# Raw score products of the second batch moved ahead of the first FFN tile, with fixed engine and load orders there

## The chip, the cores and the metric

The kernel runs on one core of a Trainium2 chip, in one launch. The metric is the device time of that launch in microseconds (us). The engines are PE (TensorE), DVE (VectorE), ACT (ScalarE), POOL (GpSimd) and SP (SyncE, which here only issues transfers).

## The reference

A channel attention is followed by a two-layer network. For each of 4 batches, q, k and v are 6080 x 256:

```python
qn = q / (np.linalg.norm(q, axis=1, keepdims=True) + 1e-06)
kn = k / (np.linalg.norm(k, axis=1, keepdims=True) + 1e-06)
s = kn.transpose(0, 2, 1) @ qn / tau          # 256 x 256 per batch
a = np.exp(s - s.max(-1, keepdims=True))
a /= a.sum(-1, keepdims=True) + 1e-09
x = (v @ a).reshape(24320, 256)
h = x @ w_in                                   # 256 -> 2048
return np.maximum(0.01 * h, h) @ w_out         # 2048 -> 256
```

The two weights arrive as 64-bit floats, which the kernel takes apart as pairs of 32-bit integers.

## The kernel before

**Stages.** The attention matrix of a batch is folded into the first weight: for each batch the kernel makes W = a w_in (256 x 2048), and then computes v W, the leaky step and the product with w_out. In the text, "batch 1" is the first one and "batch 2" the second (`scores[0]` and `scores[1]` in the code, b = 0 and b = 1).

**Scores.** q and k of a batch are read in 48 chunks of 128 rows, two to a group (`G = 2`, 24 groups; `Scores.load`, L124). A chunk's product k^T q adds into one PSUM bank (`product`, L168). It has two forms. Raw: the float32 chunk goes into the matmul as it is, two matmuls, each of which the trace shows as two records. Split: ScalarE rounds the chunk to a shorter format (`cast`, L157), VectorE takes what is left (`low`, L162), and six matmuls multiply high and low halves. Beside it each chunk is squared on ScalarE (`square`, L151) and added up on VectorE (`add_square`, L154), for the norms. When all chunks are in, a chain follows: sums, norms, rows, scaling, exponentials, transposes (`norms_mm` to `turned_low`).

**Weights.** A block of 128 x 512 64-bit numbers is converted (`f64_split`, L320) by six VectorE and three ScalarE instructions, with the loads in `Conversions.load`. There are 8 blocks of w_in and 8 of w_out. Converted w_in blocks are also stored to memory for later batches (L371). `w_product` (L395) multiplies a column block j of w_in by the attention matrix (two times six matmuls), `w_taken` copies it to SBUF, and `w_parts` (L417) forms the sums and the high and low halves of the stationary blocks for pairs 2j and 2j+1.

**FFN tiles.** The 6080 columns of a batch's v are cut into 6 tiles (five of 1024 columns, as two halves of 512, and one of 960), 24 tiles in all; tile 0 is the first tile of batch 1. A tile runs over 8 pairs p of the hidden blocks. A pair is a Strassen-Winograd step of seven block products of three matmuls (`block_product`, L546), with copies of PSUM to SBUF on ScalarE (`taken`, L574), additions on VectorE (`add`, L569) and the leaky step with its split into halves (`leaky`, L557). The 24 matmuls with w_out for a pair (`ffn_out`, L583) are spread through the next pair by `out(n)`. v is split by `v_parts` (L520) one tile ahead.

**Order.** A tile framework orders the instructions of each engine; `in_order` (L99) adds an edge from the last instruction that was noted for an engine. In the tile loop (L854) the main sequence is written out; side work is put in queues by engine (`put`, L630) and taken out by `slot(queue, room)` (L621): as many entries as their given lengths fit into the room. `at(w, fn)` attaches work to pair number w of the whole run. A batch's score chunks (`chunk_work`, L652) are attached while the batch before is in its tiles.

**The start before.** All 24 groups of batch 1 are multiplied raw, with four weight conversions in between (L787 to L796). Then the first 5 groups of batch 2 (`FILL = 5`, 10 chunks) are multiplied raw and squared while the chain of batch 1's softmax runs (L797 to L842), with no order between most of these steps beyond the ones that `issue_after` states; v of tile 0 is split; W's first column block is made. The other 12 conversions are attached to pairs 0 to 5, two to each, as whole runs (`convert`, L741), and column blocks 1 to 3 of W to pairs 0 to 5 (`w_early`, L698). The remaining 38 chunks of batch 2 take the split form, spread over 25 pairs from pair 8 on (L752 to L758).

**Buffers.** `v_split` (10 buffers) holds the raw groups of batch 1, early w_in blocks and v's halves; `g_split` (5) squares and later the leaky halves; `qk_split` (3) two square sums and later chunk halves; `w_split` (4) W's blocks for one pair each; `raw` (4) 64-bit blocks, raw groups and w_in blocks.

Of the kernel before, what the change touches and what calls it, by code (L numbers as in the profile page):

```python
# [19 lines left out]
G = 2  # L20
# [3 lines left out]
FILL = 5  # L24
# [7 lines left out]
def channel_attention_ffn(  # L32
# [77 lines left out]
    class Scores:  # L110
# [78 lines left out]
        def sums(self):  # L189

            acc, other = self.acc
            nc.vector.tensor_tensor(out=acc, in0=acc, in1=other, op=ALU.add)
            nc.vector.tensor_tensor(out=acc[:, :, 0, :], in0=acc[:, :, 0, :], in1=acc[:, :, 1, :], op=ALU.add)
            self.acc = [acc[:, :, 0, :]]

# [118 lines left out]
    def f64_load(bits):  # L314

        raw = ld.tile([P, TW, 2], I32, name="f64_raw", tag="raw", bufs=RBUFS)
        nc.sync.dma_start(out=raw.rearrange("p n w -> p (n w)"), in_=bits.bitcast(I32))
        return raw

    def f64_split(raw, hi, lo):  # L320
        low, high = raw[:, :, 0], raw[:, :, 1]
        scale, x = temp(I32, "f64_scale"), temp(I32, "f64_x")
        nc.vector.tensor_scalar(
            out=scale, in0=high, scalar1=20, scalar2=0x7FF, op0=ALU.logical_shift_right, op1=ALU.bitwise_and
        )
        nc.vector.tensor_scalar(out=x, in0=high, scalar1=0xFFFFF, scalar2=None, op0=ALU.bitwise_and)
        nc.scalar.activation(out=scale, in_=scale, func=AF.Relu, bias=exp_bias[:, 0:1], scale=2.0**23)
        tail = low.bitcast(F32)
        nc.scalar.activation(out=tail, in_=low.bitcast(U32), func=AF.Copy, scale=2.0**-52)
        nc.vector.scalar_tensor_tensor(  # L330
            out=scale, in0=high, scalar=-(2**31), in1=scale, op0=ALU.bitwise_and, op1=ALU.bitwise_or
        )
        x32 = x.bitcast(F32)
        nc.vector.scalar_tensor_tensor(out=x32, in0=x, scalar=2.0**-20, in1=tail, op0=ALU.mult, op1=ALU.add)
        nc.vector.scalar_tensor_tensor(
            out=x32, in0=x32, scalar=1.0, in1=scale.bitcast(F32), op0=ALU.add, op1=ALU.mult
        )
        nc.scalar.copy(out=hi, in_=x32)
        nc.vector.tensor_tensor(out=lo, in0=x32, in1=f32(hi), op=ALU.subtract)

    class Conversions:
# [5 lines left out]
        def load(self):  # L347
            bits, split = self.blocks.pop(0)
            self.loaded.append((f64_load(bits), split))

        def split(self):
            raw, split = self.loaded.pop(0)
            split(raw)
# [3 lines left out]
    win = {}  # L357
# [9 lines left out]
    def win_block(j, h, early):  # L367
        def split(raw):
            w = win[j, h] = win_tile(early)
            f64_split(raw, w[:, 0, :], w[:, 1, :])  # L370
            nc.sync.dma_start(out=win_dram[j][h], in_=flat(w))  # L371

        return w_in[h * P:(h + 1) * P, j * TW:(j + 1) * TW], split
# [41 lines left out]
    w_sums = {}  # L415

    def w_parts(b, j):  # L417
# [25 lines left out]
        for k in range(2):  # L443
# [24 lines left out]
            def rest(k=k, p=p, blocks=blocks, store=store):  # L468
                last = split(k, blocks(S1, 4, "w_rest"), S1, (s12, S1, 2), (s34, S3, 2))
                store(S1, 4)  # L470
                if b == 0:
# [18 lines left out]

    def wo_block(i):
        fs = slice(i * FPB, (i + 1) * FPB)

        def split(raw):
            f64_split(raw, *(wo[x][:, fs, :].rearrange("p f d -> p (f d)") for x in range(2)))

        return w_out.rearrange("(f p) d -> p f d", p=P)[:, fs, :], split
# [5 lines left out]
    def v_load(i):  # L503
# [3 lines left out]
        src = vT[b].rearrange("(h p) n -> p h n", p=P)[:, :, t * TILE:t * TILE + 2 * w]  # L507
        for h in range(CH):
            nc.sync.dma_start(out=raw[:, h, :, 0:w], in_=src[:, h, :].rearrange("p (j n) -> p j n", j=2))
        v_raw[i] = raw  # L510
# [72 lines left out]
    def ffn_out(i, p):  # L583
# [4 lines left out]
        f1 = f2 + 2  # L588
        if p == 0:
# [62 lines left out]
    def chunk_work(sc, j):  # L652
# [4 lines left out]
        if j == 0:  # L657
            sc.begin([acc_tile()], bank("s"))
            put("act", 0.6, lambda: sc.square(0, sc.acc[0]))
# [37 lines left out]

    def w_early(j, h):  # L698


        def taken():
            ins = w_taken(0, j, h)
            if h == CH - 1:
                for _, fn in w_parts(0, j):
                    with in_order("dve"):
                        issued["dve"] = fn()
            return ins

        put("pe_late", 1, lambda: w_product(0, j, h, "y"), [("act", 0.6, taken, (), True)])

# [11 lines left out]
    for i in range(NTILES):  # L722
        w = i * NPAIR
        if i + 1 < NTILES:
            at(w, v_load, i + 1)
            at(w + 2, v_begin, i + 1)
            at(w + 4, v_work, i + 1, 2, 7)
            at(w + 7, v_work, i + 1, 7, 11, True)
# [7 lines left out]
    win_blocks = [[win_block(j, h, j < 2) for h in range(CH)] for j in range(NWC)]  # L736
    conv = Conversions(win_blocks[0] + win_blocks[1] + [
        x for j in range(NWC) for x in wo_blocks[2 * j:2 * j + 2] + (win_blocks[j + 2] if j + 2 < NWC else [])
    ])

    def convert(n):  # L741
        for _ in range(n):
            conv.load()
        for _ in range(n):
            conv.split()

    for w in range(6):
        at(w, convert, 2)
    for b in range(1, B):
        w0 = (b - 1) * WPB  # L750
        sc = scores[b]
        done = FILL * G if b == 1 else 0  # L752
        begin_at, span = (NPAIR, 25) if b == 1 else (2, 31)
        when = {j: w0 + begin_at + (j - done) * span // (NCHUNK - done) for j in range(done, NCHUNK)}
        for i in range(done // G, len(sc.groups)):
# [18 lines left out]
    def load_ahead(i):  # L774
        if i < n0:
            after["load"] = sc.load(i, work.tile([P, 2, G, C], F32, name="qk_raw0", tag="v_split", bufs=VBUFS))
            with tc.issue_after(after["load"].ins):
                if i in EARLY_LOAD:
                    conv.load()
                if i == n0 - 1:  # L780
                    v_load(0)
# [5 lines left out]
    for i in range(n0):  # L787
# [5 lines left out]
        for j in sc.groups[i]:  # L793
            sc.product(j)
        if i in EARLY_SPLIT:
            conv.split()  # L796
    sc.sums()  # L797
    sc.norms_mm()
    sc.norms_taken()
    sc.norms_begun()  # L800
    after["dve"] = sc.norms()
    with tc.issue_after(after["load"].ins):
        for i in range(min(2, FILL)):
            nxt.load(i, qk_raw())
    sc.rows_mm()
    sc.rows_taken()
    after["scaled"] = sc.scaled()
    sc.exps()
    after["normed"] = sc.normed()
    nxt.begin([acc_tile()], bank("s"))  # L810
    filled = []

    def fill(n):
        for i in range(len(filled), min(len(filled) + n, FILL)):
            for j in nxt.groups[i]:
                nxt.product(j)
                if j == 0:
                    nxt.square(j, nxt.acc[0])
                else:
                    sq = temp(name="sq").rearrange("p (x c) -> p x c", x=2)  # L820
                    nxt.square(j, sq)
                    nxt.add_square(sq)
            if i + 2 < FILL:
                nxt.load(i + 2, qk_raw())
            filled.append(i)

    with tc.issue_after(after["dve"].ins):
        fill(2)
    sc.turn("x")
# [96 lines left out]
```

## Time and profile before

| what | value |
|---|---|
| median of 3 runs | 2223.62 us (2222.81 to 2224.13) |
| the profiled execution, first to last instruction | 2225.9 us |
| its mean granted TensorE clock | 0.990 |
| PE busy | 2174.0 us (98%) |
| DVE busy | 1488.5 us (67%) |
| ACT busy | 1483.2 us (67%) |
| first copy of tile 0's outputs (ACT, L609) | 209.4 us after the start |
| mean DMA rate | 146 GB/s |

The page is one execution, seen by the hardware profiler. Busy time is the union of an engine's instructions, and a busy PE need not be at full rate: the granted clock stands in a line of its own. In the page's second part the span is cut in 40 slices, and each digit is a busy share in tenths. A group of instructions has its line, engine, form, count, busy time, mean length in ns, and the idle time of the engine ahead of it with what ended it. A table of stages has for each stretch the length, the busy time of PE, its weight loads (PEld), DVE, ACT and POOL with the count of instructions, the granted clock, the share of the DMA engines and GB/s. In the list of waits stand the total, the count and the longest.

### The profile page before, as it was taken

The numbers are of one execution on the slowest core, as the hardware profiler recorded it, in microseconds if no ns is written. First come the engines' busy times: TensorE is split into PE (matmuls) and PEld (weight loads), VectorE is DVE, ScalarE is ACT, GpSimd is POOL, SyncE is SP. The second block draws the span as 40 slices with busy tenths as digits, with TensorE's granted clock in tenths as the row PEclk, the third lists the DMA queues.
The fourth block names the chain that finished last, engine by engine and source line by source line (L and its number), as shares of the span: only waits on it lengthen the run. The fifth ranks groups of instructions, "written<-read, shape, count | busy, mean of one in ns | idle before, by whom it ended". The sixth has DMA issues, their size and how long they took to land.

```text
span 2225.9 us, 27253 instructions
## 1 busy us (share of the span) xinstructions
PE 2174.0 (98%) x9940; PEld 1814.1 (81%) x9940; DVE 1488.5 (67%) x2651; ACT 1483.2 (67%) x2563; POOL 2.8 (0%) x10
## 2 busy tenths in 40 slices
PE   9679999999999999999999999999999999999999
PEld 7467888888888888888887888888888888888887
DVE  7986667666766776666766667676677655556554
ACT  6556777766657777776656777777665666666665
POOL 0000000000000000000000000000000000000000
PEclk9889999999999999999999999999999999999999
DMA  9435343342753434433464344343354432332331
GB/s 347 145 142 200 121 155 134 130 157 83 241 204 112 156 123 145 154 116 138 147 227 156 119 159 159 115 155 129 121 192 156 146 137 83 138 121 100 119 118 36
DMA packets 98967, 324.74 MB, mean 146 GB/s; under 512 B 10257, under 2 KB 22033, under 8 KB 98833
## 3 DMA queue, kind: packets, MB, share of 16 engines
q1 hardware_dynamic: 98832, 323.00, 42.1%
q8 instruction: 78, 1.28, 0.2%
q14 instruction: 57, 0.46, 0.1%
HBM read 264.50 MB, written 58.46 MB: 145 GB/s over the span
## 4 chain that ended last, share of the span: by engine, by line
PE 89%; DVE 5%; DMA 3%; ACT 2%; issue 0%; SPq 0%; ACTq 0%; DVEq 0%
PE ps_o L597 44%; PE ps_x L551 22%; PE ps_z L551 11%; PE ps_y L551 5%; PE ps_s L182 5%; PE ps_s L401 1%; DMA qk_raw<-in_k_dram 1%; DVE h L572 1%; DVE g_split L565 1%; DMA w_dram<-w_rest 1%; ACT h L562 1%; ACT g_split L563 1%; DMA f_raw<-in_w_out_dram 1%; DMA qk_raw<-in_q_dram 1%; DVE v_split L516 0%
## 5 line engine op out<-in xcount | busy, mean ns | idle before, releaser
L597 PE MATMUL ps_o<-g_split,w_out_split 128*128 128x512 f32 (+1 forms) x4608 | 1165.5, 388 | 0.0
L597 PEld LDWEIGHTS ps_o<-g_split,w_out_split 128*128 128x128 f32 x4608 | 867.7, 188 | 175.5
L565 DVE TENSOR_TENSOR g_split<-h,g_split 128x512 fp32r<-128x512 f32 (+1 forms) x768 | 525.0, 684 | 395.3 <-ACT g_split L563 394.4
L551 PE MATMUL ps_x<-v_split,w_split 128*128 128x512 f32 (+1 forms) x2304 | 653.7, 392 | 29.4 <-DVE w_split L439 16.2
L562 ACT ACTIVATE h<-h 128x512 f32<-128x512 f32 (+1 forms) x576 | 361.8, 628 | 292.3 <-DVE h L572 292.3
L578 ACT COPY h<-ps_x 128x512 f32<-128x512 f32 (+1 forms) x576 | 334.3, 580 | 312.4 <-PE ps_x L551 311.7
L551 PEld LDWEIGHTS ps_x<-v_split,w_split 128*128 128x128 f32 x2304 | 423.7, 189 | 114.0 <-ACT h L578 12.4
L563 ACT CAST g_split<-h 128x512 fp32r<-128x512 f32 (+1 forms) x768 | 473.4, 616 | 23.9
L572 DVE TENSOR_TENSOR h<-ps_z,h 128x512 f32<-128x512 f32 (+1 forms) x384 | 262.0, 682 | 284.7 <-ACT h L578 278.0
L551 PE MATMUL ps_z<-v_split,w_split 128*128 128x512 f32 (+1 forms) x1152 | 324.4, 390 | 6.3 <-DVE h L572 6.3
L551 PEld LDWEIGHTS ps_z<-v_split,w_split 128*128 128x128 f32 x1152 | 216.5, 188 | 52.5 <-DVE h L572 8.1
L551 PE MATMUL ps_y<-v_split,w_split 128*128 128x512 f32 (+1 forms) x576 | 162.9, 391 | 0.6 <-ACT w_a L411 0.6
L572 DVE TENSOR_TENSOR h<-ps_y,h 128x512 f32<-128x512 f32 (+1 forms) x192 | 131.3, 684 | 0.6
L551 PEld LDWEIGHTS ps_y<-v_split,w_split 128*128 128x128 f32 x576 | 109.0, 190 | 23.5 <-ACT w_a L411 1.1
L182 PEld LDWEIGHTS ps_s<-qk_split 128*128 128x128 f32 x804 | 114.1, 190 | 11.3 <-issue 1.0
L562 ACT ACTIVATE h<-ps_x 128x512 f32<-128x512 f32 (+1 forms) x192 | 112.8, 587 | 10.8 <-PE ps_x L551 10.8
L182 PE MATMUL ps_s<-qk_split 128*128 128x256 f32 x804 | 118.1, 283 | 0.0
L160 ACT CAST qk_split<-qk_raw 128x512 fp32r<-128x512 f32 x134 | 82.9, 619 | 31.8 <-PE ps_s L182 24.0
L516 DVE TENSOR_TENSOR v_split<-v_raw,v_split 128x512 fp32r<-128x512 f32 (+1 forms) x144 | 98.7, 686 | 4.7
L155 DVE TENSOR_TENSOR sq_acc<-sq_acc,sq 128x512 f32<-128x512 f32 x141 | 96.2, 683 | 0.0
L164 DVE TENSOR_TENSOR qk_split<-qk_raw,qk_split 128x512 fp32r<-128x512 f32 x134 | 91.6, 684 | 2.3 <-ACT qk_split L160 2.3
L152 ACT ACTIVATE sq<-qk_raw 128x512 f32<-128x512 f32 x141 | 88.8, 633 | 2.0 <-DMA qk_raw<-in_k_dram 2.0
(101 smaller groups left out, 726.7 us busy)
## 6 DMA issues: line engine op xcount, KB each, us to landing
w_split<-w_dram SPq DMA_DIRECT2D x184, 896.0 KB, 4.7
qk_raw<-in_q_dram SPq DMA_DIRECT2D x92, 256.0 KB, 3.6
qk_raw<-in_k_dram SPq DMA_DIRECT2D x92, 256.0 KB, 3.8
v_raw<-in_vT_dram SPq DMA_DIRECT2D x40, 512.0 KB, 4.9
out_dram<-o_sb SPq DMA_DIRECT2D x80, 256.0 KB, 4.2
win<-win_dram SPq DMA_DIRECT2D x24, 512.0 KB, 4.1
w_dram<-w_rest SPq DMA_DIRECT2D x24, 512.0 KB, 3.1
w_dram<-w_first SPq DMA_DIRECT2D x24, 384.0 KB, 3.4
```

The lines of the kernel that those rows point to most:

```text
L152: return nc.scalar.activation(out=out, in_=self.chunk(j), func=AF.Square)
L155: return nc.vector.tensor_tensor(out=self.acc[0], in0=self.acc[0], in1=sq, op=ALU.add)
L164: return nc.vector.tensor_tensor(out=sp[:, :, 1, :], in0=self.chunk(j), in1=f32(sp[:, :, 0, :]), op=ALU.subtract)
L182: mm = nc.tensor.matmul(out=s, lhsT=lhsT, rhs=rhs, start=False, stop=last and n == len(passes) - 1, skip_group_check=True,)
L516: last = nc.vector.tensor_tensor(out=sp[:, 1, 0:w], in0=src, in1=f32(sp[:, 0, 0:w]), op=ALU.subtract)
L551: mm = nc.tensor.matmul(out=ps[:, 0:n], lhsT=w[:, x, a, :], rhs=sp[:, y, 0:n], start=first and k == 0, stop=k == 2, skip_group_check=True,)
L562: nc.scalar.activation(out=out[:, 0:n], in_=h[:, 0:n], func=AF.Prelu, alpha=0.01)
L563: issued["act"] = nc.scalar.copy(out=sp[:, 0, 0:n], in_=out[:, 0:n])
L565: issued["dve"] = nc.vector.tensor_tensor(out=sp[:, 1, 0:n], in0=out[:, 0:n], in1=f32(sp[:, 0, 0:n]), op=ALU.subtract)
L572: issued["dve"] = nc.vector.tensor_tensor(out=h[:, 0:n], in0=ps[:, 0:n], in1=h[:, 0:n], op=ALU.add)
L578: issued["act"] = nc.scalar.copy(out=h[:, 0:n], in_=ps[:, 0:n])
L597: issued["pe"] = nc.tensor.matmul(out=o_ps[i][j][h][:, 0:n], lhsT=wo[x][:, f, h * P:(h + 1) * P], rhs=sp[:, y, 0:n], start=p == 0 and earl ...
```

## The change

- `FILL` goes from 5 to 18: 36 chunks of batch 2 are multiplied raw ahead of tile 0. Their loads go to buffers that are unused at that time (`spare`), in a fixed order on SP with v and the weight blocks.
- The last 12 chunks of batch 2 are multiplied raw too, in tile 0: five in pair 0, one in each later pair.
- No chunk of batch 2 is squared ahead of tile 0. Its 48 squares are taken from a second load of q and k, in 25 pairs from pair 8 on; nothing is cast, subtracted or multiplied there.
- Order of the start: a helper `run` puts each instruction behind the last one on its engine, so that VectorE, ScalarE, PE and SP there have the order that is written.
- A conversion becomes seven steps (`f64_steps`). At the start they are interleaved by hand for six blocks (the first four of w_out and w_in's third column block); in tile 0 the last six are queue entries, each step putting the next.
- W's column block 1 is multiplied ahead of tile 0 and cut in its queue; blocks 2 and 3 are made in pairs 0 and 1 and pairs 3 and 4. Their parts are queued in the order `FIRST`, which puts pair 2j's first half ahead of the sums.
- Stores of the four early w_in blocks wait in a list: one is issued in the middle of the start, three behind the last loads.
- In v's split for tile 0 the cast goes to ScalarE. In tile 0 alone the slots have more room.

The diff, cut to its core (`FIRST` is (2, 0, 1, 3, 4, 5)):

```diff
-FILL = 5
+FILL = 18
...
+    def run(engine, fn, *args):
+        with in_order(engine):
+            issued[engine] = ins = fn(*args)
+        return ins
...
+        return [("dve", 0.85, fields), ("act", 0.72, power), ("act", 0.7, floats), ("dve", 0.7, sign),
+                ("dve", 1.4, value), ("act", 0.65, upper), ("dve", 0.7, lower)]
...
+        def store():
+            w = win[j, h] = win_new[j, h]
+            stores.append(lambda: nc.sync.dma_start(out=win_dram[j][h], in_=flat(w)))
+            if j > 1:
+                stores.pop()()
...
-        nc.vector.tensor_copy(out=sp[:, 0, 0:w], in_=src)
+        if i:
+            nc.vector.tensor_copy(out=sp[:, 0, 0:w], in_=src)
+        else:
+            with in_order("act"):
+                issued["act"] = nc.scalar.copy(out=sp[:, 0, 0:w], in_=src)
...
+                parts = list(w_parts(0, j))
+                if j == 2:
+                    for x in FIRST:
+                        put("dve", *parts[x])
+                else:
+                    run("dve", parts[FIRST[0]][1])
+                    for x in reversed(FIRST[1:]):
+                        put("dve", *parts[x], (), True)
...
-    for j in range(1, NWC):
+    for j in range(2, NWC):
         for h in range(CH):
-            at(2 * j - 2 + h, w_early, j, h)
+            at(3 * j - 6 + h, w_early, j, h)
...
-    for w in range(6):
-        at(w, convert, 2)
+    for w in (0, 0, 2, 3, 4, 5):
+        at(w, convert, w > 0)
...
-        for j in range(done, NCHUNK):
-            at(when[j], chunk_work, sc, j)
+        for j in range(NCHUNK):
+            at(when[j], square_work if b == 1 else chunk_work, sc, j)
...
+    def spare(i):
+
+        if i < 3:
+            t = work.tile([P, 2, NS, P], F32, name="qk_raw1", tag="w_split", bufs=4)
+            return t.rearrange("p x s f -> p (x s f)")[:, 0:2 * G * C].rearrange("p (x g c) -> p x g c", x=2, g=G)
+        if i < 8 or 11 <= i < 16:
+            return work.tile([P, 2, G, C], F32, name="qk_raw1", tag="g_split", bufs=GBUFS)
+        return work.tile([P, 2, G, C], F32, name="qk_raw1", tag="qk_split", bufs=3)
...
+    fill(3)
+    run("dve", sc.sums)
+    run("pe", sc.norms_mm)
+    conv_begin()
+    conv_do(0, 2)
+    run("dve", sc.norms_taken)
...
+    run("pe", sc.turn, "x")
+    conv_do(0)
+    v_do(1)
+    run("sp", stores.pop(0))
+    run("act", sc.turned_high)
...
+    for h in range(CH):
+        run("pe", w_product, 0, 1, h, "yz"[h])
+        run("act", w_taken, 0, 1, h)
+    v_do(3)
+    conv_do(3, 2)
+    conv_begin()
+    conv_do(4, 2)
+    conv_do(3)
+    fill(2)
+    v_do(5)
+    conv_do(4, 2)
+    conv_begin()
+    conv_do(5, 2)
+    conv_do(4)
+    fill_load(1)
+    fill(1)
+    parts = list(w_parts(0, 1))
+    for x in FIRST:
+        put("dve", *parts[x])
+    conv_do(5, 3)
+    fill_load(3)
+    while stores:
+        run("sp", stores.pop(0))
+    for j in range(FILL * G, NCHUNK):
+        w = max(0, j - NCHUNK + NPAIR)
+        if w and j % G == 0:
+            at(w - 1, lambda i=j // G: nxt.load(i, spare(i)))
+        at(w, put, "pe", 1, lambda j=j: nxt.product(j))
...
-            slot("act", 0.65)
+            slot("act", 0.65 if i else 0.75)
...
-            slot("pe", 1)
+            slot("pe", 1 if i or p else 3)
...
-            slot("dve", 2.2)
+            slot("dve", 2.2 if i else 3.6)
...
-            slot("act", 1.8)
+            slot("act", 1.8 if i else 2.2)
...
-            slot("dve", 1.3)
+            slot("dve", 1.3 if i else 2.8)
...
+            if i == 0:
+                slot("dve", 1.5)
```

More of the change, by code (lines that the diff above doesn't have):

```diff
@@ L367, in win_block, with halves @@
     def win_block(j, h, early):
[L368 to L373, printed above, removed]
+        def halves():
+            w = win_new[j, h] = win_tile(early)
+            return w[:, 0, :], w[:, 1, :]
+        def store():
[3 more added lines that the diff above has]
+                stores.pop()()
+        return w_in[h * P:(h + 1) * P, j * TW:(j + 1) * TW], halves, store
     def win_load(j):
@@ L413, in w_taken @@
         return ins
-    w_sums = {}
+    w_done = set()
     def w_parts(b, j):
@@ L470, in rest @@
                 store(S1, 4)
+                w_done.add((b, p))
                 if b == 0:
@@ L775, in load_ahead @@
         if i < n0:
[L776 to L781, printed above, removed]
+            run("sp", sc.load, i, work.tile([P, 2, G, C], F32, name="qk_raw0", tag="v_split", bufs=VBUFS))
+            if i in EARLY_LOAD:
+                run("sp", conv.load)
     for i in range(AHEAD):
@@ L793, in channel_attention_ffn @@
         for j in sc.groups[i]:
-            sc.product(j)
+            issued["pe"] = sc.product(j)
         if i in EARLY_SPLIT:
             conv.split()
[L797 to L809, printed above, removed]
@@ L811, in channel_attention_ffn, with fill_load @@
+    def fill_load(n):
+        for i in range(len(nxt.raw), len(nxt.raw) + n):
+            run("sp", nxt.load, i, spare(i))
     filled = []
     def fill(n):
-        for i in range(len(filled), min(len(filled) + n, FILL)):
+        for i in range(len(filled), len(filled) + n):
             for j in nxt.groups[i]:
[L816 to L824, printed above, removed]
-            filled.append(i)
@@ L827, in channel_attention_ffn @@
[L827 to L842 removed]
+                run("pe", nxt.product, j)
@@ new lines, in fill, with conv_begin, conv_do, v_do @@
+            filled.append(i)
+    running = []
+    def conv_begin():
+        running.append(deque(conv.steps()))
+    def conv_do(n, steps=1):
+        for _ in range(steps):
+            engine, _, fn = running[n].popleft()
+            run(engine, fn)
+            while running[n] and running[n][0][0] == engine:
+                run(engine, running[n].popleft()[2])
+    def v_do(n):
+        for fn in v_tile[:n]:
+            run("dve", fn)
+        del v_tile[:n]
+    fill_load(4)
+    run("sp", v_load, 0)
@@ new lines, in channel_attention_ffn @@
+    v_tile = [fn for _, fn in v_parts(0)]
+    fill_load(1)
+    run("sp", conv.load)
+    fill_load(2)
+    run("sp", conv.load)
+    fill(3)
[4 more added lines that the diff above has]
+    run("dve", sc.norms_taken)
+    run("dve", sc.norms_begun)
+    run("dve", sc.norms)
+    fill(3)
+    fill_load(2)
+    run("sp", conv.load)
+    run("pe", sc.rows_mm)
+    conv_begin()
+    conv_do(1, 2)
+    run("dve", sc.rows_taken)
+    run("dve", sc.scaled)
@@ new lines, in channel_attention_ffn @@
+    conv_do(1)
+    v_do(1)
+    fill(2)
+    fill_load(2)
+    run("sp", conv.load)
+    parts = [list(w_parts(0, j)) for j in (0,)]
+    for x in FIRST:
+        run("dve", parts[0][x][1])
+    conv_do(2, 2)
+    conv_begin()
+    conv_do(3, 2)
+    conv_do(2)
+    fill(2)
+    fill_load(2)
+    for h in range(CH):
+        run("pe", w_product, 0, 1, h, "yz"[h])
+        run("act", w_taken, 0, 1, h)
+    v_do(3)
+    conv_do(3, 2)
+    conv_begin()
+    conv_do(4, 2)
+    conv_do(3)
+    fill(2)
```

155 lines of the change are left out of this document (92 added, 63 removed).

## The prediction

> **What bounds the kernel now.** I read the page first, then a table of stages whose borders I set at three events: the end of batch 1's score products, the first FFN product, and the first product of the second tile. The page gives the span and shows that TensorE idles, and loses its clock, only near the start:
>
> ```profile
> span 2225.9 us, 27253 instructions
> ...
> PE   9679999999999999999999999999999999999999
> ...
> DVE  7986667666766776666766667676677655556554
> ...
> PEclk9889999999999999999999999999999999999999
> ```
>
> A slice is 55.6 us; slices two to four (up to 223 us) are where PE is below 9, and DVE is fullest there. The table of stages (length, then busy time of PE, PEld, DVE, ACT, POOL, the granted clock, DMA share and GB/s):
>
> ```profile
> 0.00:48.70 48.70, 44.61 (x195) 38.01 (x195) 36.72 (x48) 33.47 (x38) 1.75 (x8) 1.00 0.97 346
> 48.70:77.50 28.80, 17.72 (x71) 13.47 (x71) 26.91 (x67) 12.65 (x25) 0.00 (x0) 0.86 0.54 191
> 77.50:202.40 124.90, 98.83 (x373) 74.54 (x374) 100.89 (x218) 70.87 (x122) 0.00 (x0) 0.88 0.44 158
> 202.40:292.90 90.50, 90.50 (x431) 76.09 (x430) 61.84 (x100) 67.44 (x118) 0.00 (x0) 1.00 0.41 138
> 1740.00:1821.60 81.60, 81.60 (x361) 67.35 (x360) 48.32 (x78) 52.91 (x92) 0.00 (x0) 1.00 0.35 119
> ```
>
> I call the five rows A to E. A: batch 1's raw scores; DMA share 0.97, PE nearly full. B: the softmax chain, 28.8 us, in which PE works 17.7 and DVE 26.9: VectorE and the dependency chain set its length. C: tile 0 takes 124.9 us with DVE busy 100.9 (81%) and PE at a clock of 0.88. D: the second tile, 90.5 us, PE without a gap. E: a tile of the last batch, which has no score work beside it, 81.6 us, again without a gap. So from 202.4 us on a microsecond of TensorE work is a microsecond of time; before that it is not.
>
> Who holds PE in C, from the waits there:
>
> ```profile
> PE ps_x L551 <- DVE w_split L439: 16.2, 4, 5.3
> PE ps_x L551 <- ACT h L578: 7.2, 7, 1.9
> PE ps_x L551 <- DVE w_split L440: 5.0, 3, 3.0
> ```
>
> 21 us are waits for VectorE to cut the weights that the next pair needs. VectorE also does most of eleven of the sixteen weight conversions in this tile (the count of L335 below).
>
> **Part 1: products leave tiles 1 to 4.** Before, 38 of batch 2's 48 chunks are cast, subtracted and multiplied as six matmuls in pairs 8 to 32. Now only their squares stay there. Price of one product, from the timeline of TensorE in the second tile (start, length, instruction), and of one three-matmul block:
>
> ```profile
> 226.76 0.88 PE L182 MATMUL ps_s<-qk_split 128*128 128x256 f32 x6
> 227.47 0.86 PE L551 MATMUL ps_x<-v_split,w_split 128*128 128x512 f32 x3
> ...
> 233.23 0.84 PE L551 MATMUL ps_x<-v_split,w_split 128*128 128x512 f32 x3
> 233.91 0.84 PE L551 MATMUL ps_z<-v_split,w_split 128*128 128x512 f32 x3
> ```
>
> From start to start a product is 0.71 us, so 38 are 27.0. The other way: D minus E is 8.9 us for 8 pairs; over the 25 pairs that is 27.8. I take 27.4. All of it lies on PE in stretches where PE has no gap, so it counts in full. What is next late there? In E VectorE is busy 48.3 of 81.6 us; all 48 squares over the same 25 pairs are 15 a tile, one ScalarE and one VectorE instruction each, against 12 chunks with two and two now, so both stay below D's 67.4 and 61.8. The squares' inputs are read a second time: D's DMA share is 0.41, and its score loads grow from 12 to 15 chunks. No cost. Term: -27.4.
>
> **Part 2: the fill before tile 0 grows from 10 chunks to 36.** A raw chunk is four records; from the long run in A, 42.77 us for 48 chunks, a group of two costs 1.78 us:
>
> ```profile
> 5.55 42.77 PE L182 MATMUL ps_o<-qk_raw 128*128 128x256 f32 x192
> 48.70 1.10 PE L173 MATMUL ps_s<-qk_raw,zeros 128*128 128x512 f32 x2 [0.37 <-DMA qk_raw<-in_k_dram]
> ...
> 77.47 0.77 PE L551 MATMUL ps_x<-v_split,w_split 128*128 128x512 f32 x1 [3.93 <-DVE w_split L439]
> ```
>
> 18 groups are 32.1 us. Two column blocks of weights (24 matmuls at 0.227, a third of the 0.68 between the last two rows above) are 5.4; before, only one block was made here. The small products (zeros, norms, rows, transposes) are between 0 and 6.1: B's 17.72 less five groups (8.9) and twelve weight matmuls (2.7), the upper end holding the cold clock; I take 4. Sum 41.5: PE runs 48.7 to 90.2 if fed, so tile 0 starts 12.7 us later than its 77.5.
>
> Is it fed? Loads first, from the SyncE timeline, the issue table and a window of A:
>
> ```profile
> 41.42 0.47 SPq L129 DMA_DIRECT2D qk_raw<-in_q_dram  x1
> ```
> ```profile
> qk_raw<-in_q_dram SPq DMA_DIRECT2D x92, 256.0 KB, 3.6
> ```
> ```profile
> 20.00:40.00 20.00, 20.00 (x95) 17.60 (x94) 19.16 (x27) 15.95 (x20) 0.52 (x1) 1.00 1.04 389
> ```
>
> A group is q and k, 512 KB. 18 groups, six weight blocks, the first tile of v and one store are 14.2 MB, 36.4 us at 389 GB/s: done near 78 when begun at 41.4, while PE wants the last at 88. A group comes every 1.35 us and is eaten every 1.78. The three remaining stores, put last on SP, wait behind the load of group 20, which needs the buffer of group 17 (about 90); one weight tile of the conversions waits for the first of them, to about 95, when VectorE would reach it anyway. So PE is the bound of the fill.
>
> VectorE in this stretch, by lengths of single instructions in C (and, from its timeline, the sums that begin the chain of the norms):
>
> ```profile
> L565 DVE TENSOR_TENSOR g_split<-h,g_split 128x512 fp32r<-128x512 f32 x31 | 21.3, 687 | 10.8 <-ACT g_split L563 10.8
> L335 DVE SCALAR_TENSOR_TENSOR f_x<-f_x,f_scale 128x512 f32<-128x512 f32 x11 | 7.4, 683 | 0.0
> L440 DVE TENSOR_TENSOR w_split<-w_s,w_split 128x256 fp32r<-128x256 f32 x16 | 6.0, 416 | 0.0
> L516 DVE TENSOR_TENSOR v_split<-v_raw,v_split 128x512 fp32r<-128x512 f32 x7 | 4.8, 691 | 0.2
> L323 DVE TENSOR_SCALAR f_scale<-f_raw 128x512 int32<-128x512 int32 x10 | 4.2, 421 | 1.0 <-DMA f_raw<-in_w_out_dram 1.0
> L439 DVE CAST w_split<-w_s 128x256 fp32r<-128x256 f32 x16 | 3.9, 284 | 0.0
> ```
> ```profile
> 50.86 1.22 DVE L192 TENSOR_TENSOR sq_acc<-sq_acc,sq_acc 128x1024 f32<-128x1024 f32 x1
> ```
>
> A conversion is two of 0.42 and four of 0.68: 3.6. Cutting one column block is about 6.9 (four sums at 0.42, then eight casts and eight subtractions between 0.22 and 0.42; mean about 0.33). The v splits of tile 0 without their casts, now on ScalarE, are 11 at 0.69: 7.6. Six conversions 21.4, one block 6.9, v 7.6, and the score chain about 10.5 (estimate: B's 26.9 less the v parts, squares and conversion steps now in it): 46.4 from 50.9, so VectorE is through at about 97.5. That is 7 us after PE has finished the fill. PE has pair 0's first two blocks and three chunks for 4 us; then it waits about 4, for the copy of `h11`, which stands behind the last conversion on ScalarE.
>
> **Part 3: tile 0.** PE's work from its first product to that of the next tile: eight pairs of 21 matmuls, seven of 24 (the last pair's outputs come later), 24 for two weight blocks: 360 at 0.227 = 81.7. Twelve raw chunks at 0.89 are 10.7. Sum 92.4; of C's 124.9 the same sum without chunks and with three blocks was 84.4, so 40.5 were lost to waits and clock. VectorE's work by lengths: 56 adds and low halves 38.5, three weight blocks 20.6, six conversions 21.4, v of tile 1 10.5: 91. Lengths overlap a little: C's groups sum to some 115 for 100.9 busy, so 91 becomes 80.
>
> The clock is where a rule has to be weighed against the trace:
>
> ```profile
> 112.72 2.13 PE L551 MATMUL ps_x<-v_split,w_split 128*128 128x512 f32 x3 [5.28 <-DVE w_split L439]
> 114.65 1.48 PE L551 MATMUL ps_y<-v_split,w_split 128*128 128x512 f32 x3
> ...
> 134.02 0.96 PE L551 MATMUL ps_x<-v_split,w_split 128*128 128x512 f32 x3 [1.23 <-ACT h L578]
> ```
>
> After a wait of 5.28 us six matmuls take 3.6 us; after one of 1.23 three take the usual 0.9. So a long wait costs about 1.9 more and a short one nothing, and I add 1.9 once, for the 4 us wait. Taking C's mean clock of 0.88 for the whole tile instead would add 12.6 and give 2197. The Trainium skill ("TensorE: Matmul & The Clock Gate", Part 1) says that the clock halves only after an idle window of about 3.4 us; by that rule the tile has one cold window at most, as I take it, and the rows agree.
>
> PE's floor for the tile's end is 90.2 + 92.4 + 4 + 1.9 = 188.5. VectorE at the density it reached in C (0.81) ends at 97.5 + 80/0.81 = 196. The weights are now cut about two pairs ahead of use, which speaks for the lower end; VectorE's nearly equal load for the upper. I take the middle, 192.3, 10.1 less than 202.4.
>
> Sum: -10.1 - 27.4 = -37.5. The profiled span of 2225.9 becomes 2188.4; the runs' median is 2223.6, 2.3 below it, so the forecast is 2186.
>
> **The rivals.**
> (a) Steps so fine that nothing waits: tile 0 ends at 90.2 + 92.4 = 182.6, and the time is 2176. For it: half of C's waits name weights that are now ready early. Against: VectorE's own 97.5 at the start.
> (b) The waits stay. In the new slots VectorE may do up to 3.6 us of queued steps between two adds that PE needs, and ScalarE 2.2; if tile 0 loses 40.5 us as before, it ends at 223.1, and the time is 2217. Against: the conversions in the tile go from eleven to six. Half of that loss gives 2197 and lies within the forecast's range.
> (c) The products' removal is worth nothing, because something else holds tiles 1 to 3 at 90.5: then 2213. D's gapless PE and E's 81.6 speak against it.
> (d) Slower: the fill is bound by its buffers. From group 8 on each load waits for a buffer that an earlier product frees, on one in-order queue that also holds conversions' loads and a store. If a group took the round of issue, landing and product, 3.6 + 1.78 = 5.4 us, for the last ten groups, the fill would end 36 us later, at 126, and the time would be 2222; with the first eight held as well, 65 us later, 2251. The change is lost from 1.78 + 37.5/18 = 3.9 us a group on. Against: five buffers of one kind and three of another let several loads be under way.
>
> **How the numbers follow.** Forecast 2186 (own range 2178 to 2198): 0.6. (a) 0.13, (b) 0.16, (c) 0.04, (d) 0.07. The range from 2175 to 2208 takes in (a) and the lower part of (b), and leaves out about 0.18. A change under 0.2% (4.4 us) cannot be told from none here, since three runs lie 1.3 us apart and the profile 2.3 from their median; (b) and (c) lie mostly beyond it on the fast side. Faster 0.91, same 0.04, slower 0.05.
>
> **What would show it.** Right: the first FFN product near 90; PE without gaps of over a microsecond from 48.7 to there at clock 1.00; the second tile's first product near 192; tiles 1 to 3 at 81.6 with no products of scores in them; conversions spread thinly on VectorE. Wrong: waits of PE for score loads in the fill (d); waits for `h` copies or adds through all of tile 0 (b); tiles 1 to 3 above 83 (c).

## The result, and the profile after

The changed kernel takes 2188.53 us (median of 4 runs, 2187.29 to 2188.85) against 2223.88 us for the kernel before in the same set of runs: a ratio of 0.9837, with a 95% interval of 0.9823 to 0.9851, or 35.4 us less. The forecast was 2186.

The page of the profile after, with the lines that answer to those of before:

```profile
span 2187.1 us, 27094 instructions
...
PE   9899999999999999999999999999999999999999
...
DVE  7787676667767676775776766677677555565554
...
PEclk9999999999999999999999999999999999999999
```

The two slices of PE below 9, the second and the third, have become one, and the clock's digit is 9 in all. VectorE, which was at 9 and 8 in these two slices, is now at 7 and 8. The table of stages of the changed kernel (columns as before), cut at its first FFN product, at the end of a wait in pair 0, and at the first products of the second and third tile:

```profile
48.80:88.96 40.16, 39.37 (x187) 33.62 (x186) 31.09 (x81) 11.56 (x22) 0.00 (x0) 1.00 1.01 374
88.96:102.70 13.74, 4.32 (x20) 3.38 (x19) 10.69 (x19) 7.30 (x13) 0.00 (x0) 0.83 0.97 342
102.70:197.82 95.12, 93.51 (x390) 74.46 (x391) 79.03 (x169) 61.85 (x107) 0.52 (x1) 0.97 0.47 168
197.82:279.50 81.68, 81.68 (x361) 67.51 (x360) 56.36 (x91) 61.64 (x108) 0.00 (x0) 1.00 0.49 163
```

The fill is dense: 39.4 of 40.2 us at a clock of 1.00, with the DMA engines full beside it. Then come 13.7 us in which PE works 4.3. The rest of tile 0 looks full, and the second tile has come down from 90.5 to 81.7 us. The timeline of TensorE in the changed kernel shows the hole:

```profile
88.96 1.04 PE L598 MATMUL ps_x<-v_split,w_split 128*128 128x512 f32 x3
89.84 0.84 PE L598 MATMUL ps_y<-v_split,w_split 128*128 128x512 f32 x3
90.53 2.75 PE L187 MATMUL ps_s<-qk_raw 128*128 128x256 f32 x12
102.70 1.65 PE L598 MATMUL ps_x<-v_split,w_split 128*128 128x512 f32 x3 [9.42 <-ACT h L625]
104.14 1.48 PE L598 MATMUL ps_z<-v_split,w_split 128*128 128x512 f32 x3
...
197.82 0.84 PE L598 MATMUL ps_x<-v_split,w_split 128*128 128x512 f32 x3
```

PE has pair 0's first two blocks and three chunks, as forecast, then waits 9.4 us for the copy of `h11`. In what follows "the third block" is the row at 102.70, and "the second tile" begins at the last row.

**Where the time went.** Trace against trace the spans differ by 38.8 us. The second tile begins at 197.8 instead of 202.4: -4.6. Tiles 1 to 4 are 28.0 shorter. Of the other 6.2, 5.9 lie in tiles 6 and 12, where a batch begins; no step of the change is there. PE's waits behind the second tile's start are, in the kernel before and then in the changed one:

```profile
PE ps_z L551 <- DVE h L572: 6.3, 3, 2.9
```
```profile
PE ps_z L598 <- DVE h L619: 3.1, 3, 1.2
```

The one in tile 6 begins where VectorE waits for the landing of a weight store from a single buffer: 5.5 us after its issue in the trace before, 4.0 in the one after. The longer wait, with the matmuls slowed behind it, makes tile 6 and tile 12 each 3 us longer. It varies between executions: the trace of e4, whose instructions there are the changed kernel's, has tile 12 at 92.4 us, as before, instead of 89.8. The profiled execution before had more of it than most; that is why the spans differ by 38.8 and the medians by 35.4.

### The profile page after: what moved, and what is told of

Read it like the earlier page. It is cut to its first block, busy times and chain, and to the rows that moved or that the text cites. A ratio compares the mean times of both kernels' runs of the same rounds, so it can differ in the third digit from the quotient of the medians.

```text
span 2187.1 us, 27094 instructions
## 1 busy us (share of the span) xinstructions
PE 2164.6 (99%) x9864; PEld 1808.8 (83%) x9864; DVE 1465.2 (67%) x2606; ACT 1465.0 (67%) x2532; POOL 3.3 (0%) x11
## 4 chain that ended last, share of the span: by engine, by line
PE 91%; DVE 3%; DMA 3%; ACT 2%; issue 0%; SPq 0%; DVEq 0%; ACTq 0%
PE ps_o L645 45%; PE ps_x L598 23%; PE ps_z L598 11%; PE ps_y L598 6%; PE ps_s L187 4%; PE ps_s L440 2%; DMA qk_raw<-in_k_dram 1%; DVE h L619 1%; ACT h L609 1%; ACT g_split L610 1%; DMA qk_raw<-in_q_dram 1%; DVE g_split L612 1%; DMA w_dram<-w_rest 1%; DMA f_raw<-in_w_out_dram 0%; DMA win_dram<-win_early 0%
## 5 line engine op out<-in xcount | busy, mean ns | idle before, releaser
L157 ACT ACTIVATE sq<-qk_raw 128x512 f32<-128x512 f32 x141 | 89.3, 633 | 0.0
L187 PEld LDWEIGHTS ps_s<-qk_split 128*128 128x128 f32 x576 | 81.7, 190 | 8.3 <-issue 1.0
L187 PE MATMUL ps_s<-qk_split 128*128 128x256 f32 x576 | 84.9, 283 | 0.0
L165 ACT CAST qk_split<-qk_raw 128x512 fp32r<-128x512 f32 x96 | 59.4, 618 | 26.0 <-PE ps_s L187 22.1
L169 DVE TENSOR_TENSOR qk_split<-qk_raw,qk_split 128x512 fp32r<-128x512 f32 x96 | 65.7, 685 | 2.3 <-ACT qk_split L165 2.3
```

The lines of the kernel that those rows point to most:

```text
L157: return nc.scalar.activation(out=out, in_=self.chunk(j), func=AF.Square)
L169: return nc.vector.tensor_tensor(out=sp[:, :, 1, :], in0=self.chunk(j), in1=f32(sp[:, :, 0, :]), op=ALU.subtract)
L187: mm = nc.tensor.matmul(out=s, lhsT=lhsT, rhs=rhs, start=False, stop=last and n == len(passes) - 1, skip_group_check=True,)
```

## The experiments

Two questions were put. What makes the 9.4 us wait, which I had put at 4? And what sets the end of tile 0: PE with its added products, or VectorE and ScalarE? Before the first runs the waits of VectorE in the changed kernel between 50.9 and 102.9 us gave the candidates for the first:

```profile
DVE f_scale L336 <- DMA f_raw<-in_w_out_dram: 5.2, 1, 5.2
DVE w_out_split L363 <- ACT w_out_split L360: 2.3, 1, 2.3
DVE win_early L363 <- ACT win_early L360: 2.0, 2, 1.3
DVE v_split L563 <- ACT v_split L562: 1.6, 2, 1.0
```

The written order puts the first conversion's first step ahead of the norms, and its block has not landed: 5.2 us with the whole chain behind it. ScalarE, in turn, waits for a buffer whose store is issued late:

```profile
ACT win_early L360 <- DMA win_dram<-win_early: 4.3, 1, 4.3
```

**e1, the norms ahead of the first conversion.**

```diff
-    conv_begin()
-    conv_do(0, 2)
     run("dve", sc.norms_taken)
     run("dve", sc.norms_begun)
     run("dve", sc.norms)
+    conv_begin()
+    conv_do(0, 2)
```

> The first weight conversion starts behind the norms instead of ahead of them, so that VectorE does not wait 5.2 us for that block's landing with the norms queued behind. In the changed kernel PE waits 9.4 us in pair 0 and the second tile begins at 197.8 us. Theory V (VectorE's queue order and the late store are two waits in parallel, the later one counts): VectorE is some 5 us earlier at first, but the fifth conversion still needs the buffer whose store lands near 98, so PE's wait stays 8 to 9.5 us and the second tile begins at 196.5 to 198. Rival L (the late landing alone makes the wait): the wait falls to about 4.5 us and the second tile begins near 192. Rival W (it is only the amount of VectorE's work in tile 0 and before it): the wait falls, but the second tile begins at 197 to 198 all the same.

Measured: 2188.85 us, one run. The second tile begins at 198.2 and PE's wait is 9.8, both just beyond theory V's ranges. The waits of PE, ScalarE and VectorE in e1:

```profile
PE ps_x L598 <- ACT h L625: 10.4, 3, 9.8
...
ACT win_early L360 <- DMA win_dram<-win_early: 4.7, 1, 4.7
...
DVE nx L219 <- PE ps_y L208: 3.2, 1, 3.2
DVE f_scale L336 <- DMA f_raw<-in_w_out_dram: 2.7, 1, 2.7
```

PE's wait is as long as before, so rival L falls. But the edit did not free VectorE. In place of the 5.2 us it waits 3.2 for PE's product of the norms, which stands behind six chunks of the fill, and 2.7 for the landing of the second block; the first step that needs both (L269) begins at 63.4 instead of 62.7. ScalarE's wait for the store is there as before.

**e2, the stores earlier.**

```diff
     conv_do(4)
+    while stores:
+        run("sp", stores.pop(0))
     fill_load(1)
...
     fill_load(3)
-    while stores:
-        run("sp", stores.pop(0))
```

> The three remaining stores of the early weight blocks are issued ahead of the load of group 17 instead of behind that of group 20; nothing else differs. Theory V: ScalarE's 4.3 us wait for the store goes, but VectorE reaches the same step only 1.3 us earlier, so PE's wait falls from 9.4 to about 8 us and the second tile begins at about 196.5. Rival S (the store alone makes the wait): the wait falls by 4 us to about 5 and the second tile begins near 193. Rival W: it begins at 197 to 198.

Measured: 2187.71 us, one run; the third block begins 0.9 us earlier, at 101.8, and the second tile at 197.2. That is rival W's number; theory V had 196.5. The timeline of PE in e2:

```profile
95.61 1.10 PE L187 MATMUL ps_s<-qk_raw 128*128 128x256 f32 x4 [2.85 <-DMA qk_raw<-in_k_dram]
101.76 1.65 PE L598 MATMUL ps_x<-v_split,w_split 128*128 128x512 f32 x3 [5.04 <-ACT h L625]
```

Rival S falls too. The stores now stand ahead of the last groups' loads, so PE waits 2.9 us for a chunk and then 5.0 for the copy; with that chunk's 1.1 the hole is 9.0 us wide instead of 9.4. The gain of 0.9 is small beside the spread of the traces: the changed kernel, e4, e6 and e9, whose instructions up to the third block on ScalarE and VectorE are the same, have that block at 102.3 to 103.5.

**e3, both.** 

> Both edits at once: the norms ahead of the first conversion, and the stores ahead of the load of group 17. Theory V: PE's wait in pair 0 falls by about 5 us to 4 to 5, the clock after it recovers sooner, and the second tile begins at 191 to 193.5. Rival W (VectorE's work in tile 0 sets its end): the wait falls by as much, but other waits take its place later in tile 0, and the second tile begins at 196 to 198.

Measured: 2186.55 us, one run; the third block at 100.7, the second tile at 196.2.

```profile
95.25 1.10 PE L187 MATMUL ps_s<-qk_raw 128*128 128x256 f32 x4 [3.40 <-DMA qk_raw<-in_k_dram]
100.68 1.65 PE L598 MATMUL ps_x<-v_split,w_split 128*128 128x512 f32 x3 [4.33 <-ACT h L625]
```

The third block gains 2.0 us, more than either edit gave alone, but theory V wanted 5. In place of the first 5.2 us VectorE still waits 1.9 for PE's norms and 1.8 for the second block, and it has a third wait, the 2.3 us for ScalarE, which e10 and e11 take up. Of the 2.0 us, 1.6 arrive at the second tile: nothing else moved in tile 0. Rival W's number (196 to 198) came, without the new waits that it wanted.

**e4, the last 12 products left out of tile 0.**

```diff
-        at(w, put, "pe", 1, lambda j=j: nxt.product(j))
```

> The changed kernel with the products of the last 12 score chunks of batch 2 left out of tile 0 (its scores lack these rows); 3 to 5 of them stood beside PE's wait, 7 in later pairs. If PE is the bound of tile 0 once the wait is over, the tile loses the 7 later chunks and the two ahead of the third block of pair 0, 8 us: the second tile begins at about 189.5 to 191. If VectorE is the bound there, PE's waits grow instead and it begins at 195 to 198. The whole time moves by the same amount.

Measured: 2189.91 us, one run; the second tile begins at 196.2. The second case came (195 to 198): PE's waits grew. The whole time did not follow, since tile 12 is 2.5 us longer in this trace. The third block begins at 103.5, later than in the changed kernel, because the first conversion's block landed 2.0 us later, which the edit does not touch. From the third block to the second tile it is 92.7 us instead of 95.1, although 9 chunks, 8 us of PE, are gone. Of these 2.4 us, 2.0 are in pair 0, behind the third block, where two chunks are gone. Pairs 1 to 7 have the same lengths to 0.1 us, but for one that lost 0.4. In pair 1 of e4 PE now waits where the chunk stood, for the copy of the block before:

```profile
114.43 0.97 PE L598 MATMUL ps_x<-v_split,w_split 128*128 128x512 f32 x3
115.24 0.85 PE L598 MATMUL ps_z<-v_split,w_split 128*128 128x512 f32 x3
115.93 1.29 PE L645 MATMUL ps_o<-g_split,w_out_split 128*128 128x512 f32 x5
117.75 0.96 PE L598 MATMUL ps_x<-v_split,w_split 128*128 128x512 f32 x3 [0.53 <-ACT h L625]
```

So the two chunks behind the third block cost their time in full, and the seven in pairs 1 to 7 cost 0.4 us together, though a trace of the changed kernel shows PE nearly without gaps there.

**e5, nearly all of the moved products left out.**

```diff
             for j in nxt.groups[i]:
-                run("pe", nxt.product, j)
+                if j == 0:
+                    run("pe", nxt.product, j)
...
-        at(w, put, "pe", 1, lambda j=j: nxt.product(j))
+        if j == NCHUNK - 1:
+            at(w, put, "pe", 1, lambda j=j: nxt.product(j))
```

> The changed kernel with the raw products of batch 2's chunks 1 to 46 left out (its scores come from two chunks); loads, buffers and every other step stay. The moved matmuls are 46 x 0.89 = 41 us of PE work in the start and tile 0. Theory V2 (VectorE and ScalarE, not PE, set the length of the start and of tile 0): the second tile begins at 190 to 197 instead of 197.8, although PE idles for most of the start and runs at a lower clock there. Rival P (the fill is PE time on the path, as my prediction's first term has it): it begins about 30 to 40 us earlier, at 158 to 168. Between them lies a mixture. The total time moves with it: 2181 to 2188 by V2, about 2150 by P.

Measured: 2187.32 us, one run. With 41 us of matmuls less the second tile begins at 195.4, 2.4 us earlier. PE's waits in e5, and the start as a stage:

```profile
PE ps_x L598 <- ACT h L625: 16.7, 7, 13.1
PE ps_y L598 <- ACT w_a L450: 8.5, 2, 8.3
PE ps_y L262 <- DVE diag L254: 7.2, 1, 7.2
```
```profile
48.80:90.00 41.20, 16.45 (x51) 11.50 (x49) 31.54 (x80) 11.86 (x23) 0.00 (x0) 0.62 1.04 381
```

PE works 16.5 of 41 us at a clock of 0.62, and the third block begins at 102.65 us, 0.05 from where it begins with them. VectorE works 31.5 us there, as in the changed kernel (31.1 in 40.2). Theory V2 holds and rival P falls: in the start and in tile 0 the moved products are all but free. (The loads of these chunks stayed, with the DMA engines full. What the loads cost was not tried.)

**e6, four conversions replaced.**

```diff
+        return [("act", 0.72, upper), ("act", 0.7, second)]
...
         def steps(self):
+            if not self.blocks and len(self.loaded) == 1 or len(self.blocks) < 4:
+                return cheap_steps(*self.loaded.pop(0))
             return f64_steps(*self.loaded.pop(0))
```

> The changed kernel with the conversions of the last four blocks of w_out (tile 0, pairs 2 to 5) replaced by two ScalarE copies each, so that these blocks hold other values: 24 VectorE and 4 ScalarE instructions fewer, 12.4 us of VectorE and about 3 us of ScalarE. Theory V2: pairs 2 to 6, now 11.2 to 13 us, fall toward PE's own length and the second tile begins 5 to 10 us earlier, at 188 to 193. Rival P2 (pairs 1 to 7 are bound by PE, whose waits there are under 1 us in all): it begins at 197 to 198.

Measured: 2186.43 us, one run; the second tile begins at 195.9, 1.9 us earlier, between the two numbers. VectorE has 12.4 us less to do in the tile and the tile does not follow: PE has 21 + 24 matmuls at 0.227 in a pair, 10.2 us, with a chunk 11.1 and with a weight block's half 12.5, and the pairs of e6 lie at 11.1 to 13.3. From the third block on the tile is 2.1 us shorter. Neither PE's work alone (e4) nor VectorE's alone (e6) is the bound.

**e7, the kernel before without its 38 split chunks.**

```diff
-        put("act", 0.6, lambda: sc.cast(j), [
-            ("dve", 0.75, lambda: sc.low(j), [("pe_next", 1, lambda: sc.product(j))]),
-        ])
+        if sc.b != 1:
+            put("act", 0.6, lambda: sc.cast(j), [
+                ("dve", 0.75, lambda: sc.low(j), [("pe_next", 1, lambda: sc.product(j))]),
+            ])
```

> The kernel before with cast, low half and product of the 38 chunks of batch 2 left out of pairs 8 to 32 (its scores lack them), squares kept: part 1 of the change alone. My term is -27.4 us, so 2196 against 2223.6, with tiles 1 to 3 at 81.6 us and the second tile's first product still near 202. A rival: part of the gain in the changed kernel's later tiles is due to the new start (other buffers, other order), then these tiles stay above 83 us and the time above 2200.

Measured: 2194.88 us beside 2222.53 for the kernel before on the same chip, 27.7 less; tiles 1 to 3 take 81.6 us each, and the second tile begins at 201.0. PE's waits in its start are those of the kernel before:

```profile
PE ps_x L551 <- DVE w_split L439: 16.5, 4, 5.3
PE ps_x L551 <- ACT h L578: 6.6, 7, 1.6
PE ps_x L297 <- DVE s_sb L288: 5.3, 1, 5.3
PE ps_x L551 <- DVE w_split L440: 5.0, 3, 3.0
```

That confirms part 1's price, and the rival falls: the later tiles need nothing of the new start.

**e8, the start without its fixed order.**

```diff
     def run(engine, fn, *args):
-        with in_order(engine):
-            issued[engine] = ins = fn(*args)
+        issued[engine] = ins = fn(*args)
         return ins
```

> The changed kernel without the edges that hold the start's instructions in the written order on each engine; the same instructions, sizes and buffers. Theory V2: PE's fill stays dense, since its products depend on loads alone, and VectorE's total is the same; the second tile begins within 5 us of 197.8. Rival O (the fixed order is what makes the start work): VectorE or PE takes up late steps first as before, waits of PE for cut weights return, and the second tile begins 8 us or more later, after 206.

Measured: 2189.66 us, one run. The second tile begins at 198.7, 0.9 us later than with the order. The fill now waits for its loads, and the first FFN product comes at 99.0, 10 us later:

```profile
PE ps_s L186 <- DMA qk_raw<-in_k_dram: 11.5, 2, 8.5
PE ps_x L597 <- ACT h L608: 0.5, 1, 0.5
PE ps_x L597 <- ACT h L624: 0.5, 2, 0.3
```

The longer of the two waits for loads is in the fill, the other, 3.1 us, in pair 0, where no wait for the copy is left. The third block comes at 106.3, 3.6 us later than with the order, but at full clock, so that the second tile is only 0.9 later. Theory V2's number came, rival O fell. (In one point its reason was wrong: the fill did not stay dense.)

**e9, e4's and e6's cuts together.** 

> Both cuts of e4 and e6 at once: the products of the last 12 chunks left out, and the last four blocks of w_out filled by two ScalarE copies each. Alone they brought the second tile's first product from 197.8 to 196.2 and to 195.9. Theory B (in pairs 1 to 7 PE's own work and the chain through ScalarE and VectorE have nearly the same length, so that cutting either leaves the other): cut together, pairs fall to PE's 10.2 us, or 11.6 with a weight block, and the second tile begins 6 to 9 us earlier, at 189 to 192. Rival C (a third thing holds the pairs, such as the order of copies in the pair itself): the cuts add up at most, and it begins at 194 to 195.

Measured: 2185.35 us, one run. The second tile begins at 193.0, 4.8 us earlier than in the changed kernel, where the two cuts alone gave 1.7 and 1.9. That is more than their sum and less than theory B's 6 to 9; half of it, 2.4, is there when pair 1 begins, and pairs 1 to 7 together lost the other 2.4. PE still waits for copies:

```profile
PE ps_x L614 <- ACT h L641: 13.2, 6, 10.7
```

10.7 of the 13.2 is the wait in pair 0, the other 2.5 fall on five later ones. Both theories missed. What holds pairs 1 to 7 when both loads are cut, the order of copies on ScalarE or the additions between them, stays open.

**e10, a first try at a better version.** On top of e3:

```diff
-        w = max(0, j - NCHUNK + NPAIR)
-        if w and j % G == 0:
-            at(w - 1, lambda i=j // G: nxt.load(i, spare(i)))
-        at(w, put, "pe", 1, lambda j=j: nxt.product(j))
+        at(0, put, "pe", 1, lambda j=j: nxt.product(j))
...
-            slot("pe", 1 if i or p else 3)
+            slot("pe", 1 if i or p else 12)
...
+    conv_do(1, 2)
+    conv_begin()
+    conv_do(2, 2)
+    conv_do(1)
+    v_do(1)
     for h in range(CH):
         run("pe", w_product, 0, 0, h, "yz"[h])
         run("act", w_taken, 0, 0, h)
-    conv_do(1, 2)
-    conv_begin()
     conv_do(2, 2)
-    conv_do(1)
-    v_do(1)
```

(The last three loads join those at the end of the start and go to buffers of `g_split`, and the later `conv_do(2, 2)` goes.)

> A version meant to beat the changed kernel, with all the work in it: e3's two edits; all of the last 12 chunks multiplied in pair 0, ahead of the third block, where PE waits; and the second and third conversions' middle steps ahead of the copies of the first weight block on ScalarE. Theory B: PE is busy through the wait (to about 101), the waits of VectorE for ScalarE near 73 go, pairs 1 to 7 keep their lengths because the other chain has them too, and the second tile begins at 192.5 to 194.5, the time is 2183 to 2186. Rival: the chunks in pairs 1 to 7 cost PE time after all, then it begins near 188 and the time is near 2179; or the longer fill only moves the wait, then it is 196 to 198 and 2187 to 2189.

Measured: 2189.07 us (5 runs, 2188.72 to 2191.26), ratio 0.9843 (0.9830 to 0.9857): no gain over the changed kernel. The second tile begins at 200.0. The timeline of PE:

```profile
91.40 1.89 PE L187 MATMUL ps_s<-qk_raw 128*128 128x256 f32 x8
97.73 11.88 PE L187 MATMUL ps_s<-qk_raw 128*128 128x256 f32 x40 [4.44 <-DMA qk_raw<-in_k_dram]
109.26 1.05 PE L598 MATMUL ps_x<-v_split,w_split 128*128 128x512 f32 x3
```

The chunks come too late: behind the stores the loads of the last groups land near 98, and then ten chunks run ahead of the third block, for which `h11` was ready at 98.5. PE keeps the written order. No number of the expectation came; the last one (196 to 198, 2187 to 2189) is nearest, with a reason that I had not seen.

**e11, the better start alone.** 

> e10 without its move of the chunks: e3's two edits, and the second and third conversions' middle steps ahead of the copies of the first weight block on ScalarE; the last 12 chunks stay where the changed kernel has them. In e10 VectorE's wait of 2.3 us near 73 was gone, but PE could not use it, for it stood waiting for late score loads and then ran ten chunks ahead of the third block. Theory V2 (VectorE's chain sets when pair 0 goes on): the third block begins some 2 us earlier than e3's 100.7, at 98 to 99.5, the second tile at 193.5 to 195.5, and the time is 2184 to 2186, some 3 us under the changed kernel's 2188.5. Rival D (the loads of the last groups set it too, since the DMA engines are full there): no earlier than e3, 196 and 2186 to 2187.

Measured: 2183.70 us (5 runs, 2182.76 to 2184.72), ratio 0.9821 (0.9807 to 0.9835). The second tile begins at 192.0. The timeline of PE in e11:

```profile
90.19 1.89 PE L187 MATMUL ps_s<-qk_raw 128*128 128x256 f32 x8
96.68 1.96 PE L187 MATMUL ps_s<-qk_raw 128*128 128x256 f32 x4 [4.60 <-DMA qk_raw<-in_k_dram]
98.71 1.65 PE L598 MATMUL ps_x<-v_split,w_split 128*128 128x512 f32 x3
100.15 0.90 PE L598 MATMUL ps_z<-v_split,w_split 128*128 128x512 f32 x3
```

The third block begins at 98.7, 4 us earlier than in the changed kernel, and without a wait for the copy: the copy and the late chunk now end together. Theory V2's number for the third block came, and rival D fell; but PE's 4.6 us are now a wait for a load, so that the loads are the next limit beside VectorE's chain. The second tile is 5.8 us earlier, 1.5 more than theory V2 had, since the clock also recovers sooner (0.90 for the second three matmuls instead of 1.48). Its times lie all below those of the changed kernel, by 4.8 us in the medians, though on another chip and with intervals of the ratio that overlap (the changed kernel's begins at 0.9823); the trace shows the 5.8 us at its place.

## Why the prediction was right, step by step

**Part 1, -27.4: right.** e7 alone gives -27.7 and the traces -28.0, with tiles 1 to 3 at 81.6 and 81.7. The squares that stayed cost nothing, as the counts of instructions said.

**Part 2, the fill ends at 90.2: right in size, wrong in what it is.** It ended at 89.0. (The page's row was misread by a slice: PE was below 9 in the second and third, up to 167 us, and not in the fourth. Nothing rests on it.) But "tile 0 starts 12.7 us later" was carried as PE's floor for the tile's end, and e5 shows that 41 us of these matmuls are worth 2.4. What sets the time up to the third block is VectorE's chain with its waits, which the prediction also had, as its second figure. Its end of the tile, 196, was 1.8 from the measured 197.8; PE's floor of 188.5 was 9.3 off. I had taken the middle. That 196 came so near is partly luck: it began 5.4 us too early (see below), and its 98.8 us for the rest of the tile were some 4 too long.

**"VectorE is through at about 97.5", then a wait of 4 us: this step failed.** VectorE was through at 102.9, and PE waited 9.4. I had added up lengths of instructions, 46.4 us, and put in no wait. From 50.9 to 102.9 the trace has VectorE busy for 39.9 us, since lengths overlap, and 11.1 us of waits: two errors, of which the smaller (6.5) hid more than half of the larger. Three were written into the order: the first conversion ahead of the norms, the late store, and conversions on ScalarE behind the copy of a weight block. I had seen the store, put its landing at about 95 and said that VectorE would come there no earlier. It landed near 98, and VectorE lost 1.3 us by it. As e1 to e3 show, taking away one wait uncovers the next: with the norms first, VectorE waits for PE's norm product and the second block instead of the first one (5.9 us in e1, 4.8 in e11, for 5.2). e11, which also moves the stores and ScalarE's conversions, gains 4 us at the third block.

**The loads: right, with less room than I gave.** I had them done near 78; group 17, the last of the fill, was issued at 76.5, and PE never waited for one in the changed kernel. Groups 19 and 20, for pair 0, were issued at 87.6 and 89.3, when their buffers came free. But the DMA engines are full through the fill (share 1.01 at 374 GB/s), and where the stores are put ahead of the last loads (e2, e3, e10, e11) PE waits 2.9 to 4.6 us for a chunk.

**The clock: one slow stretch as forecast, a little small; the rule does not fit every wait.** I took 1.9 us once, from 3.6 us for six matmuls; the rows' lengths overlap, and from start to end it was 3.4. Behind the wait of 9.4 us six matmuls took 2.7 us from start to start, where 1.4 is usual, and the next two chunks 2.9 instead of 1.8; together some 2.5. The rule that I had weighed is the Trainium skill's ("TensorE: Matmul & The Clock Gate", Part 1): half clock only after an idle window of about 3.4 us. Several waits fit it: after 2.85 (e2), 3.07 (e8) and 3.40 us (e3) a chunk took 1.10 us, after 4.60 (e11) 1.96. Others do not. In tile 6 of the kernel before, the clock fell to 0.50 behind a wait of 2.59 us, and six matmuls took 2.60 us where the changed kernel's took 1.47:

```profile
659.19 1.10 PE L551 MATMUL ps_z<-v_split,w_split 128*128 128x512 f32 x3 [2.59 <-DVE h L572]
660.09 2.60 PE L597 MATMUL ps_o<-g_split,w_out_split 128*128 128x480 f32 x6
```

**Part 3: the end of tile 0 was forecast 5.5 us too early.** The wait above was 5.4 longer than the 4 in PE's floor. The floor missed some 4 more: from the third block on the tile took 95.1 us where PE had 88.4 of work and some 2.5 of slow clock. Of the 4.2 that are left 1.6 are short waits; the others stay open. Taking the middle of floor and VectorE's sum made up for that. That PE and VectorE would both be close to the bound was right; e4 and e6 show that cutting one alone brings the second tile forward by at most 1.9 us, and e9 that cutting both gives 4.8.

**The sum.** -4.6 instead of -10.1, -28.0 instead of -27.4: -32.6 in these two places against -37.5. The medians show -35.4; the remainder lies at the two batch starts, which vary and which I had not forecast. So the 2188.5 that was measured lies 2.5 us from the forecast partly by luck: the two terms alone were 4.9 us too large. Rivals (c) and (d) are excluded, by e7 and by the dense fill. (a) and (b) did not come: the loss in tile 0 is 16.5 us (108.9 less 92.4), about 40% of the earlier 40.5, which lies between them.

## What to carry to other kernels

In a stretch where another engine's chain sets the pace, work for the idle engine is nearly free, as long as nothing that the chain needs stands behind it (in e1 VectorE waited 3.2 us for a small product behind six moved chunks). The gain of moving it there is what it cost where it came from; price both places by themselves. An order that is written out by hand turns every wait in it into a wait of all that stands behind: put first what has its inputs, and count the waits for landings and buffers along the chain and not only the lengths. An engine without gaps is not thereby the bound: leave its work out and see whether the stretch gets shorter.

## What the runs showed of the hardware

With one core at work, the DMA engines moved 374 to 383 GB/s through 40 us of loads and a few stores (the changed kernel, e5, e10); in the changed kernel PE was busy for 39.4 of 40.2 us beside it, at a clock of 1.00. The clock was at 0.50 behind waits of PE of 4.33 us (e3) and more. Behind one of 3.07 us (e8) it stayed at 1.00, but it fell to 0.50 behind waits of 2.59 us (the kernel before, tile 6) and 2.24 us (e7), so in these traces the length of the wait alone does not decide.
